# Gate scores of a recurrent attention kernel: 128 stationary columns in half of the array's rows, in place of 64x64 corners

## The chip, the core and the metric

The kernel runs on one core of a Trainium2 chip. A core has five engines with queues of their own: TensorE (PE in the profile, its weight loads PEld), VectorE (DVE), ScalarE (ACT), GpSimdE (POOL), and SyncE (SP), which issues the DMAs. The metric is the time of one execution in microseconds on the device. TensorE multiplies a stationary operand, which a load puts into its array of 128 rows and 128 columns, with a moving operand that streams through; the array can be used as a whole or in parts, of which each product names its own. Results go to PSUM, in banks of 512 fp32 numbers for each partition; VectorE and ScalarE read them there.

## What is computed

Four sequences of 768 steps, 8 heads of 40 numbers each, run through a recurrence with a matrix as its state; its output is the input of a gated MLP.

```
for t in range(S):                       # S = 768, state (B, H, D, D), D = 40
    y[:, :, t] = einsum('bhd,bhde->bhe', r_t, state)
    Sa = einsum('bhde,bhe->bhd', state, a_t)
    state = state * w_t[:, :, None, :] - einsum('bhd,bhe->bhde', Sa, b_t) \
            + einsum('bhd,bhe->bhde', v_t, k_t)
x = y, heads side by side                # (4, 768, 320)
h = gelu(x @ w_in); u, v = halves of h   # 1024 wide
out = x + (u * (w_sg @ normalised(v) + b_sg)) @ w_out
```

## The kernel before

The recurrence is cut into 12 chunks of 64 steps (`NCH`, `C`). Within a chunk the steps become matrix products: the decays w are multiplied up along the chunk, k, a and b are scaled by them, and the scores between the steps of a chunk, a 64x64 matrix for each head, give a triangular system that has to be inverted. For one chunk c and one batch b the 8 heads lie in two halves: heads 2p in partitions 0 to 63, heads 2p + 1 in partitions 64 to 127, for p = 0 to 3.

What is done for one (c, b), 48 times in all, is called a gate here, in seven pieces (`gate_1`, `gate_2`, `gate_3`, `gate_4`, `gate_a`, `gate_n`, `gate_k`; lines 248 to 301). `gate_1` to `gate_3` multiply up the decays on VectorE and write the scaled k and b side by side into one tile, `kb` (128 partitions, then pair p, then x = 0 for k and 1 for b, then 64 steps), and the scaled a into `at`. `gate_4` (line 273) is TensorE's: for each pair p and half h it multiplies k and b of that half with the scaled a of the same head, and then transposes all of `kb`. The results lie in two PSUM banks, `ab0` for the first half and `ab1` for the second: in columns 0 to 255 the scores with k (partitions 0 to 63) and with b (partitions 64 to 127), in columns 256 to 511 the transposes. `gate_a` masks the k scores on VectorE, `gate_n` writes the negated b scores into `nts` on ScalarE, where the inversion starts, and `gate_k` copies the transposes to `kbt`.

The chain from chunk to chunk (`chain1` to `chain5`, lines 417 to 497) is TensorE's too, with ScalarE and VectorE between its steps: `ru` (the right side and, with the inverse `xt`, the solution), `sp` (the new state, with `tp` its transpose), `ut`, `pq` and `yp` (the output). The inverse is built by VectorE and GpSimdE in steps on `x` with the products `tv` and `tg`, and by TensorE's `gp` and `xp`.

Every engine keeps the order in which the program is written (`InOrder`, line 112). That order comes from tables of positions: `EX`, `EW` and `T2` for the first chunks, and `GPOS` for the pieces of later gates among the chain's steps. The MLP's weights are prepared beside the last chunks, and its products (`hu`, `hv`, `sg`, `op`) follow, most of them after 400 us. A slower program for inputs out of range follows under a condition that doesn't hold here.

Every operation is recorded through one helper, so all have line 122 in the profile, and tiles tell them apart. A product of fp32 operands stands in the trace as two records, with a weight load each: `ab<-at,kb` has 1,536 records for 768 products, 32 for one gate. A transpose stands as one record, 4 for one gate. In a row's shape, `64*64 64x64` is rows and columns of the stationary operand, then partitions and columns of the moving one.

Of the kernel before, what the change touches and what calls it, by code (L numbers as in the profile page):

```python
# [18 lines left out]
C = 64  # L19
# [107 lines left out]
def engines(tc):  # L127
    nc = tc.nc
    return tuple(InOrder(tc, e) for e in (nc.vector, nc.scalar, nc.gpsimd, nc.tensor, nc.sync))
# [6 lines left out]
def attention(tc, a, xd, flag, keep, ps, mlp=None):  # L136
# [3 lines left out]
    V, A, G, T, Q = engines(tc)  # L140
    with ExitStack() as ctx:
# [101 lines left out]
        def ent(c, b):  # L243
            return (4 * c + b) % RING
# [28 lines left out]
        def gate_4(c, b):  # L273
            kb, at = gate.pop((c, b)), ats[ent(c, b)]
            ab = gate[c, b] = ps("ab0"), ps("ab1")
            for p in range(NP):
                for h in range(2):
                    r = slice(64 * h, 64 * h + 64)
                    for x in range(2):
                        T.matmul(ab[h][64 * x:64 * x + 64, C * p:C * p + C], lhsT=kb[r, p, x], rhs=at[r, p, 1],  # L280
                                 start=True, stop=True, tile_position=(64 * h, 64 * x), skip_group_check=True)
            for p in range(NP):
                T.transpose(out=ab[p // 2][:, 256 + 128 * (p % 2):384 + 128 * (p % 2)], in_=kb[:, p], identity=ident)

# [238 lines left out]
        def spread(fs, lo, hi):  # L523
            return [(lo + (hi - lo) * k / len(fs), f) for k, f in enumerate(fs)]

        PIECES = gate_1, gate_2, gate_3, gate_4, gate_a, gate_n, gate_k

        def early(c, at, X, EA, EK, w):
# [590 lines left out]
```

## Time and profile before

| | us |
|---|---|
| timed runs, median of 3 | 654.51 (654.24 to 656.18) |
| profiled execution | 661.78 |
| its span, first to last instruction | 660.0 |
| TensorE busy, products / loads | 551.5 / 493.2 |
| VectorE busy | 513.5 |
| ScalarE / GpSimdE busy | 383.3 / 372.3 |
| TensorE's mean granted clock, share of full speed | 0.905 |

The profiled execution is 7.3 us longer than the median of the timed runs; both stand here, and durations of parts come from the profiled one. Busy time counts products from the start that the profile gives to an end that it models, and products of different parts of the array overlap, so records of 218 ns can follow each other at a few ns. An idle engine's wait is put down to what ended it; "issue" says that nothing in the profile did.

### The profile page before, as it was taken

How to read it: one execution, taken by the hardware profiler on the slowest of the kernel's cores; microseconds unless marked ns; L12 is line 12 of the kernel's file. 1: busy time of each engine (PE TensorE's matmuls, PEld its weight loads, DVE VectorE, ACT ScalarE, POOL GpSimd, SP SyncE). 2: the span in 40 equal slices, each digit the busy share in tenths (PEclk: the TensorE clock that was granted, in tenths of full speed). 3: DMA queues.
4: the chain of work that ended last, by engine and by line, in shares of the span. 5: the costliest groups of instructions: out<-in, count | busy, mean ns of one | idle time of the engine just before them, and what ended most of it. 6: DMA issues, size and time to landing. Idle time of an engine off the chain costs nothing.

```text
span 660.0 us, 26858 instructions
## 1 busy us (share of the span) xinstructions
PE 551.5 (84%) x11190; PEld 493.2 (75%) x11190; DVE 513.5 (78%) x1107; ACT 383.3 (58%) x1106; POOL 372.3 (56%) x834
## 2 busy tenths in 40 slices
PE   6417878888998889888877691969999999999996
PEld 5315766776876768777767581959999999999996
DVE  7857878879888897798887659786679988767743
ACT  5627687876987778688774744564245334424410
POOL 5588587886867878678882546353322433333320
PEclk9756699989899997999978786979999999999999
DMA  7812244344344443332444331340006222000001
GB/s 234 254 58 77 78 105 109 113 121 112 99 109 112 122 117 95 97 101 76 118 110 137 83 104 55 106 129 16 31 12 199 73 89 71 32 31 0 31 25 42
DMA packets 60515, 60.77 MB, mean 92 GB/s; under 512 B 36256, under 2 KB 50336, under 8 KB 60384
## 3 DMA queue, kind: packets, MB, share of 16 engines
q1 hardware_dynamic: 60384, 58.96, 31.4%
q8 instruction: 90, 1.47, 1.0%
q14 instruction: 41, 0.34, 0.2%
HBM read 51.07 MB, written 7.86 MB: 89 GB/s over the span
## 4 chain that ended last, share of the span: by engine, by line
PE 57%; DVE 20%; ACT 10%; issue 7%; POOL 3%; DMA 1%; DVEq 0%; ACTq 0%; POOLq 0%
PE sg L122 15%; PE op L122 7%; PE hu L122 7%; PE hv L122 6%; PE ab L122 5%; PE yp L122 5%; PE pq L122 4%; PE ru L122 3%; DVE sc L122 3%; DVE x L122 2%; PE sp L122 2%; DVE at L122 2%; ACT nts L122 2%; DVE fixed L122 2%; ACT xt L122 2%
## 5 line engine op out<-in xcount | busy, mean ns | idle before, releaser
L122 POOL TENSOR_TENSOR tg<-x,n 128x56 f32<-128x56 f32 (+20 forms) x333 | 125.1, 376 | 55.4 <-ACT rhsb L122 15.3
L122 POOL TENSOR_TENSOR x<-x,tg 128x56 f32<-128x56 f32 (+20 forms) x333 | 128.2, 385 | 26.1
L122 POOL TENSOR_TENSOR gx<-g,gy 128x384 fp32r<-128x384 f32 x31 | 32.1, 1037 | 85.9 <-ACT gy L122 85.9
L122 PE MATMUL yp<-pqs,kbt 128*64 128x64 f32 x768 | 55.6, 247 | 20.2 <-DVE pqs L122 15.8
L122 PE MATMUL sg<-wsh,vh 128*128 128x384 f32 x192 | 66.3, 345 | 4.9 <-ACT vh L122 4.9
L122 PE MATMUL sg<-wsh,vl 128*128 128x384 f32 x192 | 66.2, 345 | 1.5 <-POOL vl L122 1.5
L122 ACT ACTIVATE nts<-ab 32x256 f32<-32x256 f32 x192 | 61.9, 323 | 8.1 <-DVE at L122 5.9
L122 PE MATMUL sg<-wsl,vh 128*128 128x384 f32 x192 | 65.8, 343 | 0.0
L122 PEld LDWEIGHTS yp<-pqs,kbt 128*64 128x64 f32 x768 | 45.1, 157 | 24.2 <-DVE pqs L122 16.4
L122 PE MATMUL pq<-rt,vut 128*128 128x128 f32 x384 | 59.9, 301 | 3.3 <-issue 1.8
L122 PE MATMUL ab<-at,kb 64*64 64x64 f32 x1536 | 41.7, 239 | 23.0 <-DVE kb L122 16.8
L122 ACT CAST gy<-g 128x384 fp32r<-128x384 f32 x32 | 16.4, 514 | 73.5 <-DVE g L122 73.5
L122 PEld LDWEIGHTS pq<-rt,vut 128*128 128x128 f32 x384 | 51.0, 205 | 8.1 <-issue 2.6
L122 PEld LDWEIGHTS ab<-at,kb 64*64 64x64 f32 x1536 | 34.2, 146 | 29.6 <-issue 14.6
L122 PE MATMUL yp<-rt,s 80*40 80x64 f32 x704 | 51.3, 244 | 0.0
L122 ACT CAST vh<-v 128x512 fp32r<-128x512 f32 x24 | 14.9, 620 | 57.9 <-DVE v L122 57.9
L122 ACT COPY vs<-sc 64x160 f32<-64x160 f32 x88 | 28.3, 321 | 32.6 <-DVE sc L122 31.6
L122 POOL TENSOR_TENSOR vl<-v,vh 128x512 fp32r<-128x512 f32 x24 | 31.3, 1305 | 22.7 <-ACT vh L122 22.7
L122 DVE TENSOR_TENSOR at<-ab,mask 64x256 f32<-64x256 f32 x96 | 35.7, 409 | 10.8 <-PE ab L122 10.2
L122 PEld LDWEIGHTS sg<-wsh,vh 128*128 128x128 f32 x192 | 36.8, 192 | 6.0 <-ACT vh L122 5.7
L122 DVE SCALAR_TENSOR_TENSOR g<-sg,gl,bt 128x384 f32<-128x384 f32 x32 | 19.6, 614 | 27.2 <-PE sg L122 25.3
L122 POOL TENSOR_TENSOR rs<-rs,mhalf 128x1 f32<-128x1 f32 x24 | 13.5, 561 | 48.4 <-DVE rs L122 45.6
(137 smaller groups left out, 1574.0 us busy)
## 6 DMA issues: line engine op xcount, KB each, us to landing
main<-main SPq DMA_DIRECT2D x88, 160.8 KB
vu<-vs SPq DMA_DIRECT2D x24, 160.0 KB
vs<-vb SPq DMA_DIRECT2D x24, 160.0 KB
rt<-rt SPq DMA_DIRECT2D x48, 80.0 KB
vut<-vt SPq DMA_DIRECT2D x24, 160.0 KB
xd<-yt SPq DMA_DIRECT2D x96, 40.0 KB
ws<-seq_w SPq DMA_DIRECT2D x20, 192.0 KB
xt<-xd SPq DMA_DIRECT2D x16, 192.0 KB
```

The lines of the kernel that those rows point to most:

```text
L122: return self.tc.keep_in_program_order(f(*a, **k))
```

## The change

In `gate_4` the loop over x goes. One product now takes all 128 columns of `kb` for a pair and a half, k and b together, as its stationary operand: 64 rows and 128 columns of the array, in place of a 64x64 corner for k and another for b. The result covers all 128 partitions of the bank, which puts the k scores and the b scores where they were.

```diff
             for p in range(NP):
                 for h in range(2):
                     r = slice(64 * h, 64 * h + 64)
-                    for x in range(2):
-                        T.matmul(ab[h][64 * x:64 * x + 64, C * p:C * p + C], lhsT=kb[r, p, x], rhs=at[r, p, 1],
-                                 start=True, stop=True, tile_position=(64 * h, 64 * x), skip_group_check=True)
+                    T.matmul(ab[h][:, C * p:C * p + C], lhsT=kb[r, p], rhs=at[r, p, 1],
+                             start=True, stop=True, tile_position=(64 * h, 0), skip_group_check=True)
```

On TensorE's queue, for one gate in the middle of the attention part, between the `ut` of a `chain3` and the `gp` of an inverse, there stood before (the shape is that of the result, and x2 says two equal products in a row):

```order
L122 MATMUL ut<-ident,vu_130 80x64 x4
L122 MATMUL ab_2073<-at_149,kb 64x64 x2
L122 MATMUL ab_2074<-at_149,kb 64x64 x2
L122 MATMUL ab_2073<-at_149,kb 64x64 x2
L122 MATMUL ab_2074<-at_149,kb 64x64 x2
L122 MATMUL ab_2073<-at_149,kb 64x64 x2
L122 MATMUL ab_2074<-at_149,kb 64x64 x2
L122 MATMUL ab_2073<-at_149,kb 64x64 x2
L122 MATMUL ab_2074<-at_149,kb 64x64 x2
L122 MATMUL ab_2073<-ident,kb 128x128 x2
L122 MATMUL ab_2074<-ident,kb 128x128 x2
L122 MATMUL gp<-x1z,nts_96 32x32 x32
```

and there stands now:

```order
L122 MATMUL ut<-ident,vu_130 80x64 x4
L122 MATMUL ab_1937<-at_149,kb 128x64
L122 MATMUL ab_1938<-at_149,kb 128x64
L122 MATMUL ab_1937<-at_149,kb 128x64
L122 MATMUL ab_1938<-at_149,kb 128x64
L122 MATMUL ab_1937<-at_149,kb 128x64
L122 MATMUL ab_1938<-at_149,kb 128x64
L122 MATMUL ab_1937<-at_149,kb 128x64
L122 MATMUL ab_1938<-at_149,kb 128x64
L122 MATMUL ab_1937<-ident,kb 128x128 x2
L122 MATMUL ab_1938<-ident,kb 128x128 x2
L122 MATMUL gp<-x1z,nts_96 32x32 x32
```

Nothing has changed its place, on this queue or another: each x2 of the two corners is one product of 128 result partitions, the transposes (`ident`) behind them are the same, and so are the waits. In the trace's records a gate's products go from 32 to 16, each with its load.

## Rows read from the trace of the kernel before

**Rows 1.** The page's part 1: engine, busy us (share of the span), instructions

```profile
PE 551.5 (84%) x11190; PEld 493.2 (75%) x11190; DVE 513.5 (78%) x1107; ACT 383.3 (58%) x1106; POOL 372.3 (56%) x834
```

**Rows 2.** Windows, tile ab: us, busy (count) of PE, PEld, DVE, ACT; clock, DMA

```profile
0.00:49.00 49.00, 12.07 (x288) 9.61 (x288) 5.91 (x16) 14.23 (x48) 0.73 0.60 184
49.00:77.00 28.00, 10.68 (x180) 8.37 (x180) 3.76 (x10) 8.89 (x30) 0.56 0.25 73
77.00:345.00 268.00, 49.67 (x1260) 38.06 (x1260) 26.02 (x70) 62.19 (x210) 0.95 0.40 106
```

**Rows 3.** Windows, all work, 77 to 345: PE, PEld, DVE, ACT, POOL, clock, DMA

```profile
77.00:345.00 268.00, 229.97 (x7913) 195.24 (x7914) 228.16 (x507) 208.58 (x667) 208.32 (x545) 0.95 0.40 106
```

**Rows 4.** Chain of waits, 77 to 345 us: shares of the stretch by line

```profile
by line: issue 12.1%; PE ab L122 11.2%; PE yp L122 9.1%; PE pq L122 9.0%; PE ru L122 5.5%; PE sp L122 4.6%; DVE at L122 4.0%; DVE x L122 3.5%; DVE fixed L122 3.3%; PE ut L122 3.0%; ACT xt L122 2.7%; DVE kb L122 2.6%; DVE pqs L122 2.2%; ACT 
```

**Rows 5.** Waits of PE, 77 to 345 us: us in total, times, longest

```profile
PE sp L122 <- issue: 4.7, 4, 2.0
PE ru L122 <- issue: 4.6, 10, 0.8
PE ab L122 <- issue: 3.8, 4, 1.6
PE yp L122 <- issue: 2.7, 3, 1.0
PE pq L122 <- issue: 1.8, 3, 1.3
PE gp L122 <- issue: 1.3, 2, 0.7
PE xp L122 <- issue: 0.8, 1, 0.8
```

**Rows 6.** Timeline, PE: start, length, work, records, [idle before <- releaser]

```profile
119.77 0.28 PE L122 MATMUL sp<-vu,kbt 128*32 128x40 f32 x8 [0.86 <-issue]
```

**Rows 7.** Windows, all work, between the ends of two stalls

```profile
115.67:119.77 4.10, 3.04 (x128) 2.38 (x127) 2.64 (x7) 3.61 (x12) 3.47 (x9) 1.00 0.61 178
278.49:282.58 4.09, 3.24 (x126) 2.92 (x127) 2.84 (x9) 3.40 (x10) 3.46 (x9) 1.00 0.25 64
```

**Rows 8.** DMA queues: packets, MB, share of 16 engines

```profile
q8 instruction: 90, 1.47, 1.0%
```

**Rows 9.** Timeline, PEld (weight loads) of pq and of one gate

```profile
120.33 0.97 PEld L122 LDWEIGHTS pq<-rt,vut 128*128 128x128 f32 x8
120.44 0.19 PEld L122 LDWEIGHTS pq<-rt,vut 128*128 128x128 f32 x1
121.42 0.56 PEld L122 LDWEIGHTS ab<-at,kb 64*64 64x64 f32 x32
121.47 0.21 PEld L122 LDWEIGHTS ab<-at,kb 64*64 64x64 f32 x8
122.04 0.42 PEld L122 LDWEIGHTS ab<-ident,kb 128*128 128x128 f32 x4
```

**Rows 10.** Tiles, PEld, 77 to 345 us: count, ns min/median/max, first and last start

```profile
L122 PEld LDWEIGHTS sp<-vu,kbt x1248: 106/113/172, 78.3 to 343.0; 128*32 128x32 f32 x179
L122 PEld LDWEIGHTS xp<-xt,gs x640: 102/106/111, 86.1 to 336.2; 64*32 64x32 f32 x160
L122 PEld LDWEIGHTS ab<-at,kb x1120: 129/135/136, 79.0 to 317.2; 64*64 64x64 f32 x187
L122 PEld LDWEIGHTS pq<-rt,vut x310: 186/192/338, 76.9 to 344.9; 128*128 128x128 f32 x155
```

**Rows 11.** Waits of DVE, 77 to 345 us

```profile
DVE at L122 <- PE ab L122: 6.5, 7, 1.8
```

**Rows 12.** Waits of PE and chain of waits, 0 to 77 us

```profile
PE ab L122 <- DVE kb L122: 15.5, 8, 6.7
by line: POOL x L122 12.1%; POOL tg L122 11.5%; ACT nts L122 8.4%; issue 7.3%; PE ab L122 5.8%; DVE x L122 5.1%; DMA main<-first 4.9%; DVE fixed L122 4.2%; DVE ex L122 4.2%; DVE kb L122 3.6%; ACT xt L122 3.5%; PE pq L122 3.3%; DVE n L122 2.
```

## The prediction

> **What bounds the kernel now.** I read the page first: TensorE is the busiest engine, with 551.5 of the span's 660.0 us, and VectorE is next with 513.5 [rows 1]. These are averages over very unlike stages, so I went to the stretches. The changed products are all issued in the attention part: of the 48 gates (one call of gate_4 for one chunk and one batch, 36 records each, of which 32 are the changed products and 4 are transposes) 8 lie before 49 us, 5 between 49 and 77, and 35 between 77 and 345; after 345 us there are none [rows 2]. In the stretch of 77 to 345 TensorE is busy for 230 us of 268 and VectorE for 228 [rows 3], so both are near their limit. The chain of waits for this stretch has 11.2% (30.0 us) on these tiles' products and transposes, and, larger than any engine's share, 12.1% (32 us) "issue", time in which the profile shows nothing waited for [rows 4]. The list of TensorE's waits says how much of that is TensorE's own: 27 waits in seven rows with "issue" as their releaser, 4.7 + 4.6 + 3.8 + 2.7 + 1.8 + 1.3 + 0.8 = 19.7 us, out of 268 - 230 = 38 us in which it stood idle [rows 3, 5].
>
> What these stalls are can be counted. Two that follow each other end at 115.67 and 119.77 (before the second, TensorE stood for 0.86 us), and between them TensorE took 128 products and 127 loads; between the ends at 278.49 and 282.58 it took 126 and 127 [rows 6, 7]. With the few semaphore instructions that the counts leave out, that is 256 instructions each time. The instruction queue moved 1.47 MB in 90 packets, 16 KB for each [rows 8]; over TensorE's 22,380 products and loads [rows 1] the 1.47 MB are 66 bytes for each, so a packet is about 256 of them. So I read the stalls as TensorE waiting for its next block of instructions: some 15,800 of them pass in the stretch [rows 3], 62 blocks, and 27 block ends stall, by 0.73 us on average. A busy engine is here also starved, and a change of the number of instructions counts as well as one of the work.
>
> **The change part by part.** Per gate it takes 16 products of 64 stationary columns and makes 8 of 128. In the trace each is a pair of records with a load each, so 64 instructions become 32. The moving columns (64 for each), the tiles written, the waits and the order of everything else stay. No other engine does a different thing.
>
> *Work of a gate.* Before, the four corners of the array run side by side, in eight rounds. The first loads stand at 121.42 and the next loads for the same corners at 121.47, about 0.055 later; 32 loads last 0.56 us, and without the last one's 0.14 [rows 10] the seven steps take 0.42, which is 0.060 each [rows 9]. The transposes behind them begin their loads at 122.04, so a gate's products hold TensorE for 0.62 us [rows 9]. For loads of 128 columns the nearest row is pq: its first load stands at 120.33 and its second at 120.44, 0.11 later, before the first product could stream; eight loads last 0.97, without the last one's 0.19 seven steps take 0.78, or 0.111 each [rows 9]. In pq the moving columns have doubled too, so the step alone doesn't say which of the two paces it; the first gap does, since it has only a load in it. Rows do not matter to a load: at the least and in the median, 32 columns take 106 and 113 ns with 128 rows (sp) and 102 and 106 with 64 (xp), while 64 columns take 129 and 135 and 128 take 186 and 192, some 0.9 ns for each further column [rows 10].
>
> So I take 0.11 for the first load in place of 0.055 and 0.111 for each of seven steps in place of 0.060: 0.055 + 7 x 0.051 = 0.41, say 0.42 us more per gate, 1.04 in all. The two halves of the rows still run side by side, because today's corners in both halves already do: four loads of about 0.055 fit a step of 0.060. The bounds: 0, if the 64 moving columns go on to set the step (it cannot fall below that, since there are still eight rounds of 64 columns); and, if the two halves took turns, 16 x 0.111 = 1.78 in place of 8 x 0.060 = 0.48, so 1.30 more. I take 0.42, by the nearest row.
>
> *What of it is on the path.* In 77 to 345 it is 35 x 0.42 = 14.7 us. TensorE takes its queue in order, and what it waits for there (x1z, xt, vu, s) mostly comes from engines that themselves work on its earlier products, so a later product makes those later too. The lower bound is the share that the gates' tiles have of the chain, 30.0 of their 49.7 us of TensorE time [rows 2, 4], 0.60, or 8.8 us. I take the whole. Also late are the masking of the scores on VectorE, which already waited 6.5 us for these tiles, and the negations on ScalarE behind it [rows 11]; both queues are in order, so the next chunk's kb and the products' masks behind them are late as well, which is why I allow no slack.
>
> Before 77 us, TensorE waited 15.5 us for kb, 8 times [rows 12]; that covers much. The granted clock was 0.73 before 49 us and 0.56 after [rows 2]; at half clock 0.42 becomes 0.84, so the five later gates cost up to 0.84 and the eight earlier some 0.6 each: about 9 us. The chain has 5.8% of 77 us, 4.5 us, on these tiles, out of 22.8 us of their work (12.07 + 10.68) [rows 2, 12], a fifth. I take 2 us, between 0 and 9.
>
> *Fewer instructions.* 35 x 32 = 1,120 go from the stretch, 4.4 blocks of 62. Two things follow. There are 4.4 fewer block ends, at 19.7 / 62 = 0.32 us each: 1.4 us. And time added inside a block that ends in a stall only fills the stall: 27 of 62 blocks do, so of the 35 gates about 15, each with up to 0.42: 6.4 us. Together 7.8; a stall shorter than 0.42 hides only its own length, so I take 6. The bounds are 0 and 19.7, all the stalls there are.
>
> The sum: 14.7 + 2 - 6 = +10.7 us. Its own range goes from 8.8 + 0 - 7.8 = +1 to 14.7 + 9 - 1.4 = +22. The profiled execution took 661.78 us (span 660.0), so it would take 672.5. The timed runs have a median of 654.51, 7.3 us less; the same difference put on them gives 665.2.
>
> The Trainium skill has a rule on this: "Runtime: NRT & Kernel Launch", section "Instruction fetch mechanics", has instructions come in 16 KB blocks of 256 and says that crossing a block's end is mostly hidden. The trace agrees on the size of a block and not on the cost, 27 stalls of 0.73 us. By the rule nothing would be filled, and the sum would be that of the second case below.
>
> **The rivals.** *The moving columns set the pace* (the other side). If a load of 128 columns into half of the rows hid behind two streams of 64, a gate would stay at 0.62 us and only the fetch would change: 15 gates in stalled blocks, each with 32 fewer instructions, which at the stretch's mean of 268 us for 15,800 instructions are 0.54 us of stream, capped by the stall; about 0.35 each, 5 us faster, 649.5. It decides where a load lasts under 0.06 us. Against it stands the first gap of 0.11.
>
> *The fetch gives nothing back.* Where a stall is a fixed time after the block end before, and the gates stand in blocks without one, +16.7 us: 671.2. For it: 35 of 62 block ends don't stall today. Against it: the gates are spread over all of them.
>
> *The fetch hides everything.* With relief near its bound of 19.7 the sum is about 0: 654.5. For it speaks that TensorE lost more to stalls than the gates add; against it, that a stall in one block cannot cover a gate in another.
>
> *The halves take turns.* 35 x 1.30 = 45.5 and some 5 more before 77 us: about 705. Against it are the four corners of today.
>
> **How the numbers follow.** I give the forecast 0.72, the fetch that gives nothing back 0.12, moving columns 0.08, the fetch that hides everything 0.05, and halves in turn 0.03. Differences under 0.3%, 2 us, count as none, since a measurement of this kernel can hardly tell them. Faster is the moving columns' 0.08; same is 0.05; slower is the rest, 0.87. The range goes from 656 to 677, the forecast's own low and high ends put on the timed median, and leaves out the two cases below it and the turns, 0.16, and a little of the forecast's tails.
>
> **What would show it.** The page after should have 768 records of ab with 128 columns in place of 1,536, loads of about 190 ns, the second load about 0.11 us behind the first, and some 1.04 us from a gate's first load to its transposes'. In 77 to 345 the sum of "issue" waits should fall from 19.7 to about 12, TensorE's busy share should rise, and the part after 345 should last as long as now. The forecast is wrong if the step stays at 0.06 (then faster), if it goes to 0.22 (then the halves take turns), or if the granted clock in the stretch leaves 0.95.

## The result, and the profile after

First measured: 662.27 us (median of 4 runs, 660.87 to 663.11) beside 655.10 of the kernel before (4 runs), ratio 1.0106 with an interval of 1.008 to 1.0133. In two later calls, 12 runs of the changed kernel beside 29 of the one before, the ratio was 1.0029 (0.9996 to 1.0061) and 1.0050 (1.0025 to 1.0076). In the first of these two calls (e5 to e8 below) two runs of the kernel before, one of e5 and one of e7 were over 1.5% above the fastest of their kernel; all ratios and medians here are without them. So the kernel became slower, rather by 2 to 3 us than by 7. The other runs of the kernel before lay between 653.6 and 663.0 in these calls; its execution profiled first, 661.78 us, was near the upper end. The changed kernel's first profiled execution took 663.11, only 1.3 us more.

The page's part 1 of the changed kernel (compare [rows 1]):

```profile
PE 574.2 (87%) x10422; PEld 516.7 (78%) x10422; DVE 514.8 (78%) x1107; ACT 383.1 (58%) x1106; POOL 372.3 (56%) x834
```

768 records of products fewer (384 products), 22.7 us more work of TensorE, and a span only 1.4 us longer. The rest must have been found in idle time. Where the work went, by tile ab in the windows of [rows 2] (PE, PEld, DVE, ACT; clock), and below it all work as in [rows 3]:

```profile
0.00:49.00 49.00, 19.06 (x160) 15.97 (x160) 6.17 (x16) 14.22 (x48) 0.66 0.64 184
49.00:77.00 28.00, 15.46 (x100) 13.00 (x100) 3.97 (x10) 8.47 (x29) 0.50 0.25 72
77.00:345.00 268.00, 67.91 (x700) 55.67 (x700) 26.17 (x70) 62.59 (x212) 0.95 0.40 106
77.00:345.00 268.00, 244.45 (x7419) 210.36 (x7419) 229.99 (x509) 209.81 (x674) 207.76 (x546) 0.95 0.40 106
```

After 77 us TensorE works 14.5 us more in the same 268 us, so its idle time went from 38 to 23.5. The clock there is the same 0.95; before 77 us it is lower than it was. One gate of the changed kernel on the line of weight loads (compare the gate in [rows 9]), and the loads' durations after 77 us [rows 10]:

```profile
128.79 0.97 PEld L122 LDWEIGHTS ab<-at,kb 64*128 64x128 f32 x16
129.83 0.42 PEld L122 LDWEIGHTS ab<-ident,kb 128*128 128x128 f32 x4
L122 PEld LDWEIGHTS ab<-at,kb x560: 182/188/188, 81.5 to 319.4; 64*128 64x128 f32 x187
```

From its first load to the transposes' first it takes 1.04 us; 16 loads, eight for each half of the rows, end after 0.97, so the halves do run side by side, and without the last load's 0.19 a step takes 0.111. The Trainium skill, "TensorE: Matmul & The Clock Gate", section "LDWEIGHTS (loading the stationary operand)", says that a load's time goes by its columns and not its rows; the trace agrees, 64 rows of 128 columns step as 128 rows do in pq.

The waits of TensorE named issue, 77 to 345 us, in the changed kernel (us in total, times, longest; compare [rows 5]), and its instruction queue [rows 8]:

```profile
PE ru L122 <- issue: 1.2, 3, 0.5
PE sp L122 <- issue: 1.1, 1, 1.1
PE xp L122 <- issue: 1.1, 2, 0.7
PE ab L122 <- issue: 1.0, 1, 1.0
PE yp L122 <- issue: 0.6, 1, 0.6
q8 instruction: 84, 1.38, 0.9%
```

They are 5.0 us in 8 waits, where 19.7 in 27 stood: 14.7 us less, the whole of the added work. Six blocks of 16 KB fewer are fetched. In the chain of waits the gates' tiles take the first place from issue [rows 4], and VectorE's masking waits for ab 12.8 us in 18 times, where it had 6.5 in 7 [rows 11]:

```profile
by line: PE ab L122 12.3%; PE pq L122 5.8%; issue 5.7%; DVE n L122 5.6%; ACT nts L122 4.8%; ACT gs L122 4.3%; DVE x L122 4.3%; PE ru L122 4.3%; DVE at L122 4.1%; PE yp L122 3.7%; ACT vs L122 3.6%; PE sp L122 3.5%; DVE fixed L122 3.3%; DVE x
DVE at L122 <- PE ab L122: 12.8, 18, 1.5
```

### The profile page after: what moved, and what is told of

It is laid out like the page before. It is cut to its first block, busy times and chain, and to the rows that moved or that the text cites. A ratio compares the mean times of both kernels' runs of the same rounds, so it can differ in the third digit from the quotient of the medians.

```text
span 661.4 us, 25323 instructions
## 1 busy us (share of the span) xinstructions
PE 574.2 (87%) x10422; PEld 516.7 (78%) x10422; DVE 514.8 (78%) x1107; ACT 383.1 (58%) x1106; POOL 372.3 (56%) x834
## 4 chain that ended last, share of the span: by engine, by line
PE 53%; DVE 23%; ACT 14%; issue 4%; POOL 3%; DMA 1%; DVEq 0%; SPq 0%; ACTq 0%; POOLq 0%
PE sg L122 15%; PE ab L122 7%; PE op L122 7%; PE hu L122 5%; PE hv L122 5%; PE pq L122 3%; PE yp L122 3%; ACT nts L122 3%; DVE n L122 3%; DVE x L122 3%; DVE sc L122 3%; PE ru L122 2%; ACT gs L122 2%; DVE at L122 2%; PE sp L122 2%
## 5 line engine op out<-in xcount | busy, mean ns | idle before, releaser
L122 PE MATMUL ab<-at,kb 64*128 64x64 f32 x768 | 69.5, 306 | 14.9 <-DVE kb L122 9.9
L122 PEld LDWEIGHTS ab<-at,kb 64*128 64x128 f32 x768 | 61.4, 213 | 21.2 <-ACT call L122 6.5
L122 PE MATMUL yp<-pqs,kbt 128*64 128x64 f32 x768 | 52.4, 240 | 20.5 <-DVE pqs L122 16.9
L122 PEld LDWEIGHTS yp<-pqs,kbt 128*64 128x64 f32 x768 | 41.8, 151 | 24.6 <-DVE pqs L122 17.4
L122 PE MATMUL pq<-rt,vut 128*128 128x128 f32 x384 | 58.3, 298 | 0.2
L122 ACT CAST gy<-g 128x384 fp32r<-128x384 f32 x32 | 16.4, 513 | 72.4 <-DVE g L122 72.4
L122 PE MATMUL yp<-rt,s 80*40 80x64 f32 x704 | 48.1, 236 | 0.0
L122 DVE SCALAR_TENSOR_TENSOR g<-sg,gl,bt 128x384 f32<-128x384 f32 x32 | 19.7, 615 | 26.7 <-PE sg L122 24.8
```

The lines of the kernel that those rows point to most:

```text
L122: return self.tc.keep_in_program_order(f(*a, **k))
```

## The experiments

Theory B: where TensorE takes instructions faster than they come, an instruction has a price of its own, and time added or instructions taken away give back waits one for one until none are left. Theory A: the work counts, the number of instructions little. Beside them, what the early gates cost and why. Ratios are to the kernel before in the same call, with 95% intervals; 11 or 12 runs each where nothing else is said.

| kernel | ratio | TensorE busy, 77 to 345 | issue waits there | 13th to 48th gate |
|---|---|---|---|---|
| before, first / again | 1 | 230.0 / 231.0 | 19.7 / 20.0 | 245.9 / 245.0 |
| changed, first / again / third | 1.0106 / 1.0029 / 1.0050 | 244.5 / 246.7 / 247.1 | 5.0 / 1.8 / 3.7 | 245.9 / 242.7 / 243.2 |
| e1 corners streamed twice | 1.0062 | 241.9 | 7.8 | 244.9 |
| e2 wide streamed twice | 1.0029 | 246.1 | 3.2 | 242.8 |
| e3 late gates wide | 1.0002 | 245.8 | 1.8 | 243.7 |
| e4 early gates wide | 1.0025 | 233.1 | 16.1 | 242.2 |
| e8 changed, early gates streamed twice | 1.0007 | 246.1 | 4.4 | 243.0 |
| e7 right sides in 64 | 0.9964 | 237.1 | 8.6 | 244.4 |
| e10 states in 64 | 0.9976 | 239.6 | 8.3 | 239.7 |
| e11 both in 64 | 0.9962 | 242.2 | 1.8 | 239.8 |
| e12 32 instructions more | 1.0161 | 231.7 | 25.4 | 254.9 |

All in us of one profiled execution each; issue waits are the sum of TensorE's rows of that name, the last column goes from the 13th gate's first load to the 48th's.

**The kernel before again (e6).**

> The kernel before once more, for its profile: the execution profiled first took 661.78 us, above all but the slowest of its later runs. If that one was an unlucky one, this execution is 653 to 660 us long, its first sg product starts some 3 to 5 us earlier than 430.9 us, and the waits named issue between 77 and 345 us are still well above 10 us (16 us stood in the kernel whose early gates alone have 128 columns). If instead the waits for instructions were the unlucky part, they are under 10 us here.

It took 657.39 us, its first sg product began at 426.6 (430.9 in the first). Its waits:

```profile
PE ru L122 <- issue: 5.7, 9, 1.2
PE sp L122 <- issue: 3.1, 5, 0.9
PE ab L122 <- issue: 3.1, 4, 1.1
PE xp L122 <- issue: 2.7, 2, 1.9
PE gp L122 <- issue: 2.1, 2, 1.2
PE yp L122 <- issue: 2.1, 3, 1.0
PE pq L122 <- issue: 1.2, 2, 1.0
```

20.0 us in 27, as in the first. The stalls belong to the kernel; what made the first execution long was not they.

What the waits are for stands in the traces. Counted with the semaphore instructions, the 193 waits of TensorE named issue in the 14 traces, 77 to 345 us, lie whole multiples of 256 instructions apart in each trace, to within one. And each of them ends 1.2 to 1.8 us (median 1.45) after a packet of 16 KB of the instruction queue has landed; the packet before the wait that ends at 119.77 [rows 6], for example, went from 116.93 to 118.30. In the kernel before, a packet starts 1.2 us (median) after TensorE has entered the block ahead of it and takes 1.2; with the 1.4 after the landing that is 3.8 of the 4.1 us of [rows 7]. TensorE enters 41 of its 63 blocks there no later than 1.7 us after the block's packet, as it does after all 27 waits; in the changed kernel it is 21 of 59.

**What paces a gate, and time without fewer instructions (e1, e2).** Both stream twice; e1 is shown, and e2 does the same to the changed kernel's products:

```diff
-                        T.matmul(ab[h][64 * x:64 * x + 64, C * p:C * p + C], lhsT=kb[r, p, x], rhs=at[r, p, 1],
+                        T.matmul(ab[h][64 * x:64 * x + 64, C * p:C * p + 2 * C].rearrange("p (y t) -> p y t", y=2),
+                                 lhsT=kb[r, p, x], rhs=bc(at[r, p, 1].unsqueeze(1), [64, 2, C]),
```

> The kernel before, its 64x64 corners kept, but each product streams its 64 moving columns twice (128 moving columns; the second 64 results are overwritten by the next pair's product or by the transposes, so the output stays the reference's). A gate then has as many instructions as before, and a step that should be as long as a step of 128 columns (0.111 us). Theory A (the step's length is all, instructions count little): a gate takes about 1.04 us as in the changed kernel and the time is that of the changed kernel, 662 within 2 us. Theory B (32 instructions less per gate are worth something of their own, because TensorE waits for blocks of instructions): the gate takes 1.04 us too, but the kernel is slower than the changed one by 1.4 us (fewer block ends alone) up to 8 us, so 663.5 to 670, and the waits named issue between 77 and 345 us are well above the 5 us of the changed kernel. If the second stream is free (loads pace the corners), a gate stays at 0.62 us and the time at 655.

> The changed kernel, each product streaming its 64 moving columns twice (128 moving columns, the second 64 results overwritten as in the corners' version). Theory A (the load of 128 stationary columns paces the changed gate, not the 64 moving columns): the step stays at 0.111 us, the gate at 1.04 us and the time at 662 within 2 us. Rival (the moving columns pace it or take part): the step goes to 0.16 to 0.22 us, a gate to 1.45 to 1.9 us, and the time up by 35 x 0.41 to 35 x 0.86 us, so 676 to 692.

One gate in each, on the line of loads, first e1:

```profile
125.34 0.86 PEld L122 LDWEIGHTS ab<-at,kb 64*64 64x64 f32 x32
126.38 0.31 PEld L122 LDWEIGHTS ab<-ident,kb 128*128 128x128 f32 x3 [0.17 <-issue]
```

and e2:

```profile
123.88 0.97 PEld L122 LDWEIGHTS ab<-at,kb 64*128 64x128 f32 x16
124.97 0.31 PEld L122 LDWEIGHTS ab<-ident,kb 128*128 128x128 f32 x3
```

In e2 a gate went from 1.04 to 1.09 us with twice the moving columns: the load paces it, so the first rival, with moving columns, is out. In e1 the shortest gates, with corners, take 1.03. The two differ in little but 32 instructions a gate, and e1 is the slower, 662.06 against 658.59 us, though its gates are a shade shorter. By the numbers as they were written e1 meets A (662 within 2) and misses B (663.5 and more). But these took the changed kernel for the one to compare with, and streaming twice also raised the clock in the early part (below), in both alike. Against e2, a comparison made after the fact, the 32 instructions are worth 3.5 us, inside B's 1.4 to 8. Time alone had already filled much: in e1, with as many instructions as before, issue waits fell from 20 to 7.8.

**Late or early gates alone (e3, e4).** `wide = 4 * c + b >= 13` in e3, `< 13` in e4; wide gates as in the change, the others corners.

> 128 columns only in the 35 gates that come after 77 us, corners in the first 13. Prediction's split: the late gates cost 14.7 - 6 = 8.7 us of the forecast 10.7, and the early ones 2; scaled to the 7.2 us that were measured: 5.9 late and 1.3 early, so 661. Theory E (the early gates, which cost 0.84 us each at the lower clock, make the measured loss, and the late ones are given back by fewer waits for instructions, as the two profiled executions suggest, where the lag was 3.0 us at 81.7 us and 0.9 us at 345 us): 655 to 657. Theory L (the late ones make all of it): 662.

> 128 columns only in the first 13 gates, corners in the 35 after 77 us. Prediction's split scaled to the 7.2 us: 1.3 us slower, 656.4. Theory E (the early gates make the loss): 658 to 662, and the lag of about 3 us that stands at 81 us in the changed kernel's trace stays to the end. Theory L (the late ones make all of it): 655.

e3: 657.36, 1.0002 (0.9978 to 1.0025). The 35 late gates cost nothing that shows: L's 662 and the prediction's 661 are out. It is theory E, though by its number just missed: its 655 to 657 were put on a median of 655, where the kernel before has 657.5 in this call. Its waits named issue:

```profile
PE xp L122 <- issue: 1.2, 1, 1.2
PE ru L122 <- issue: 0.3, 1, 0.3
PE yp L122 <- issue: 0.3, 1, 0.3
```

e4: 658.54, 1.0025 (0.9996 to 1.0054), 16.1 us of issue waits still there. Its 13th gate began at 72.4 us, as late as in the changed kernel (72.5, 72.4, 73.2), where before had 70.7 and 69.8. So what loss there is lies with the early gates, 1.6 us by the ratio, at E's low end, in an interval that just includes no loss. E also had the lag stay to the end, and that does not show: the 48th gate begins at 314.6 in e4, at 318.4, 315.1 and 316.4 in the changed kernel, and at 316.6 and 314.9 in the kernel before, whose own two executions differ as much. Where in the span the last 2 to 3 us are lost is open.

**The changed kernel again, and the early clock (e5, e9, e8).** e8 streams the first 13 wide gates twice.

> The changed kernel once more, in more runs and beside kernels of this call. Where the two halves of the change add up (the runs with 128 columns in the late gates alone, 1.0002 of before, and in the early gates alone, 1.0025): 1.003 of before, some 2 us slower. Where they do not add up, or the first measurement (1.0106 from 4 runs) holds: 1.008 or more, 5 us or more. The waits named issue between 77 and 345 us are 2 to 5 us in either case.

> The changed kernel a third time, in a further call. If the loss is the sum of its parts (0.0 from the late gates, 1.6 us from the early ones; 1.003 the second time), 1.001 to 1.005 of before. If the first measurement, 1.0106 from four runs of each, is right and the second one was low: 1.008 or more.

> The changed kernel with the moving columns streamed twice in the first 13 gates alone (results as before). The load paces the step, so the second stream costs no time by itself. Theory C (in the changed kernel the granted clock between 15 and 77 us is 0.50, lower than before, because TensorE streams less there; that makes the early part late by some 3 us): the clock there is 0.66 to 0.88 as in the version with all gates streamed twice, the 13th gate starts at 69.5 to 70 us in place of 72.5, and the kernel is 2 to 4 us faster than the changed kernel. Rival (the early part has slack, its clock costs nothing at the end): the time of the changed kernel within 1 us.

The repeats gave 660.15 and 660.47 us beside 659.50 and 658.14; 1.0029 and 1.0050 by ratio, or 1.9 and 3.3 us. The parts, 0 and 1.6, add up to that within the intervals. All work from 15 to 77 us (PE, PEld, DVE, ACT, POOL; clock), first of e6, the kernel before:

```profile
15.00:77.00 62.00, 32.49 (x826) 26.41 (x827) 47.50 (x106) 37.12 (x120) 43.04 (x116) 0.59 0.44 120
```

of e5, the changed one:

```profile
15.00:77.00 62.00, 38.49 (x587) 32.55 (x586) 44.41 (x99) 34.34 (x111) 41.47 (x110) 0.51 0.44 122
```

and of e8:

```profile
15.00:77.00 62.00, 32.35 (x663) 26.88 (x660) 46.17 (x104) 36.25 (x117) 42.67 (x115) 0.73 0.42 120
```

The granted clock is 0.51 in the changed kernel, which is the lower level of 1.2 GHz nearly throughout, and 0.73 with the second stream; the 13th gate comes at 70.5 in place of 72.4. The kernel took 658.66, 1.5 us less than e5 in the same call, short of C's 2 to 4 and over its rival's 1; 1.0007 (0.9978 to 1.0036) and 1.0029 overlap, so the time doesn't prove it. The traces show the lag at the 13th gate gone; at the 48th, 313.5 beside 315.1, the difference is within what one kernel's executions show. Kernels with the early gates of before have 0.54 (e3, e7) to 0.59 there, so the 0.50 to 0.51 of wide loads (e4, e5, e9) stand below them all, but not by much.

**Fewer instructions elsewhere (e7, e10, e11).** Gates stay corners. e7 changes `chain1`, e10 in the same way `chain3` (one product of `kbt[:, l0:l0 + 64]` in place of two), e11 both:

```diff
+            w = 64 if c else 32
-                for x in range(4):
-                    r = slice(32 * x, 32 * x + 32)
-                    T.matmul(ru[r, D * p:D * p + D], lhsT=at[0:k, p, x // 2, 32 * (x % 2):32 * (x % 2) + 32],
-                             rhs=vs[0:k, p, x // 2], start=True, stop=True, tile_position=(0, 32 * x), skip_group_check=True)
+                for x in range(128 // w):
+                    r, y = slice(w * x, w * x + w), w * x // 64
+                    T.matmul(ru[r, D * p:D * p + D], lhsT=at[0:k, p, y, w * x - 64 * y:w * x - 64 * y + w],
+                             rhs=vs[0:k, p, y], start=True, stop=True, tile_position=(0, w * x), skip_group_check=True)
```

> The kernel before with its gates' corners kept, but the right sides (chain1, tile ru from vs and at) of chunks 1 to 11 as products of 64 stationary columns in place of two of 32: 32 instructions less in each of 44 groups, nearly as many as the change takes from its gates. 16 loads of 64 columns last 0.55 us in yp, 32 of 32 columns some 0.28 in ru, so each group costs about 0.22 us more, 9.7 us in all, where a gate costs 0.42. Theory B (fewer instructions give back what TensorE waits for blocks, up to 16 us): 9.7 - 16 = 6 us faster than before, 651.5 beside 657.5, waits named issue under 5 us. Theory A (instructions count little): 5 to 10 us slower, 663 to 667.

> The kernel before with its gates' corners kept, and the products of the state (chain3, tile sp) as 64 stationary columns in place of two of 32: 32 instructions less in each of 44 groups. 32 loads of 32 columns last 0.37 us there, 16 of 64 columns 0.55 in the right sides, so +0.18 us a group, 8 us in all. Theory B (blocks of instructions): the waits named issue fall from 20 to about 9 us as they did with the right sides in 64 columns, and the kernel is 0.995 to 0.999 of before. Theory A (instructions count little): 1.010 to 1.012.

> Right sides and states both in 64 columns, gates in corners as before: 64 instructions less per chunk and batch, 9.7 + 8 = 17.7 us more of TensorE's work. If what fewer instructions give back is bounded by the stalls there are (20 us, of which 8.6 were left with the right sides alone), the second half buys at most 8.6 - 2 = 6.6 us for 8: the kernel is 0.5 to 3 us slower than with the right sides alone, 0.998 to 1.001 of before, waits named issue 2 to 4 us. If each block of instructions saved is worth the same without a bound, it is twice as good as the right sides alone: 0.993.

e7: 657.03 beside 659.50, 0.9964 (0.9927 to 1.0002), with 6 us more work of TensorE. A's 5 us slower is out; B has the sign, at 2.5 us by the medians in place of 6, in an interval that just includes no gain. Its issue waits:

```profile
PE sp L122 <- issue: 2.6, 4, 1.0
PE yp L122 <- issue: 2.3, 3, 1.2
PE ab L122 <- issue: 1.9, 1, 1.9
PE ru L122 <- issue: 1.6, 4, 0.6
PE gp L122 <- issue: 0.2, 1, 0.2
```

8.6 us, where B had under 5; they fell by 11.4, more than the 6 us of work could fill. e10: 0.9976 (0.9953 to 1.0000), 8.3 us, as B had it. e11: 656.38 beside 658.14, 0.9962 (0.9932 to 0.9992), faster than before and than the changed kernel; two waits are left:

```profile
PE yp L122 <- issue: 1.1, 1, 1.1
PE sp L122 <- issue: 0.7, 1, 0.7
```

Twice the saving did not give twice the gain (656.38 beside e10's 656.27): what can be given back is bounded by the stalls. The bound's own number, 0.998 to 1.001, was missed on the fast side; the 0.993 of no bound lies at the interval's very edge. In e10 and e11 the 48th gate comes some 5 us sooner after the 13th, and the kernel ends only 2 us sooner; what takes the rest back after 311 us was not followed up.

**More instructions (e12, 6 runs).** In the late gates of the kernel before, ahead of the transposes:

```diff
+            for i in range(8 if 4 * c + b >= 13 else 0):
+                h, y = i % 2, i // 2
+                r = slice(64 * h, 64 * h + 64)
+                T.matmul(ab[h][32 * y:32 * y + 32, 256:264], lhsT=kb[r, 0, 0, 0:32], rhs=at[r, 0, 1, 0:8],
+                         start=True, stop=True, tile_position=(64 * h, 32 * y), skip_group_check=True)
```

> The kernel before, its corners kept, with 8 products of 32 stationary and 8 moving columns more in each of the 35 gates after 77 us, into columns that the transposes overwrite: 32 instructions more per gate, as many as the change takes away there. Their own time, from xp (64 loads of that form begin within 0.54 us): 16 of them 0.135 us, 4.7 us in all. Theory B (between two waits for instructions 256 pass in 4.1 us, 16 ns each, and a gate's 32 are worth 0.51 us wherever TensorE is behind): 35 x 0.51 = 17.9 us where every block is behind, 7.8 where only the 27 of 62 blocks that stall today are, so 8 to 18 us slower than before, and the waits named issue up from 20 to 24 to 33 us. Theory A (only the work counts): 0 to 4.7 us slower, the waits named issue at or under 20 us.

669.39 us beside 659.17 (11 runs), 1.0161 (1.0120 to 1.0203). B's 8 to 18 us holds, A's 4.7 does not:

```profile
PE ru L122 <- issue: 9.2, 11, 1.8
PE sp L122 <- issue: 7.1, 5, 3.3
PE yp L122 <- issue: 3.6, 4, 1.4
PE ab L122 <- issue: 2.3, 5, 0.7
PE xp L122 <- issue: 1.5, 2, 0.8
PE pq L122 <- issue: 1.1, 2, 0.7
PE gp L122 <- issue: 0.6, 2, 0.4
```

The sum is 25.4 us in a window that holds fewer gates than before, since the gates come later. But the products' own time was put too low. One gate (compare [rows 9]):

```profile
128.64 0.81 PEld L122 LDWEIGHTS ab<-at,kb 64*64 64x64 f32 x48
129.47 0.42 PEld L122 LDWEIGHTS ab<-ident,kb 128*128 128x128 f32 x4
```

The shortest gates hold TensorE for 0.83 us in place of 0.63, 7.0 us in 35 gates; were it all on the path, A would come close below the interval, which begins at 7.9 us. What speaks against A is e1. From the 13th gate to the 48th, TensorE's busy time rose by 12.0 us in e1, the issue waits fell by 11 to 12 (to 7.1 from 19.2 and 18.0), and the stretch, 244.9, was no longer than before; in e12 busy time rose by 8.7, the waits by 2.5 to 3.7 (to 21.7), and the stretch by 9 to 10. In this stretch time alone is taken up by the waits, and time that comes with instructions is not. (The 4 us that e1 loses all the same lie elsewhere and were not located.) Over 1,120 instructions the 10.2 us are 9 ns each, their own work included.

## Why the prediction was right in sign, and where it was off

*What bounds the kernel.* Right: TensorE is bound by its work and by the arrival of its instructions together. e12 added instructions, and the waits rose in spite of the work that came with them; e7 took instructions away from another place, and they fell by more than its added work. That the waits are for blocks of 256 rested on the counts of [rows 7]; the packets' times in all the traces (under e6) bear it out.

*Work of a gate.* Right. 0.42 was forecast; the shortest gates went from 0.625 to 1.038 us, 0.413. The 35 later gates added 14.5 to 17 us of TensorE's busy time, against 14.7.

*The early gates.* Not contradicted at 2 us: e4 has 1.6, in an interval that just includes no loss. What the forecast didn't have is that their clock would fall too, from 0.59 to 0.51; with the wide loads the gates there went from about 1.06 to 1.9 us (medians).

*Fewer instructions.* This step failed. The term was -6, its bound -19.7, and about 12 us of waits were to be left, where 5.0 were; the waits fell by 14.7 in the first pair and by 16 to 18 in the repeats. Two assumptions made it small. First, that only the blocks whose end shows a wait have a stall to fill, 15 of the 35 gates at 0.42. In the trace of before 15 gates do lie in such blocks, but 24 lie in blocks after which TensorE went on no later than 1.7 us behind the next packet, as it does after a wait. That these too were held by the fetch is the likeliest reading, and 24 x 0.42 are 10 us; e1 shows that time added in every gate, without one instruction less, took 12 us out of the waits. Second, a saved instruction was priced over all blocks, 1.4 us for 4.4 of them. Where TensorE is behind, [rows 7] had the price: 256 in 4.1 us, 16 ns each, 0.51 us for a gate's 32, which with 0.42 of work is 0.93 us a gate and 33 us for 35, more than all stalls there were; at the 9 ns of e12 it is still 25. So the bound was the better guess, and the rival in which the fetch hides everything, given 0.05, is what the late gates did: e3, 1.0002.

*The sum.* With sizes from the middle of those measured: 15.5 + 2 - 16 = +1.5 us, beside 1.9 and 3.3 us in the repeats and 7.2 in the first four runs. The profiled pair differs by 1.3 us where the forecast had 10.7, and nearly all of that is the error of the one term. The time 665.2 came out only 2.9 us above the 662.27 first measured by luck, because another error ran against it: the execution of before that was profiled was a long one, and its 7.3 us over the median were taken off, while the changed kernel's profiled execution (663.11, not 672.5) lies 0.8 us above its own median. Why the first four runs gave 7 us, and why runs of one kernel differ by up to 10, was not found.

*The rule of the Trainium skill* ("Runtime: NRT & Kernel Launch", section "Instruction fetch mechanics", crossing a block's end is mostly hidden) does not hold in this stretch: by it e12 would have cost at most its own 7.0 us, in place of 10.2, and e7 would have been slower.

*The rivals with moving columns and with halves in turn* fell by the gate's 1.04 us and by e2.

## What to carry to other kernels

Where a queue of small products waits with nothing named as releaser, count the instructions between two such waits; if it is one number and its multiples, look for the packets of the instruction queue, price an instruction at no more than that pace (16 ns here; e12's came to 9 with their own work), and count added work there as free until the waits are used up. Take instructions out where a wider load costs least: 32 instructions cost 0.42 us of TensorE in the gates, and by an estimate from the loads' rows about 0.2 in the right sides and the states; the late gates alone came out at 1.0002, the right sides and states together at 0.9962 (0.9932 to 0.9992). Measure a change of half a per cent in more runs than four.

## What was not expected of the hardware

The same products, streamed twice, ran sooner: between 15 and 77 us the granted clock was 0.51 with 64 moving columns per load of 128 and 0.73 with 128, and TensorE's busy time fell from 38.5 to 32.4 us. And TensorE lost 20 us in 268 to waits that all end 1.2 to 1.8 us after a packet of its instructions landed, while that queue's packets took only 1.0% of the DMA engines' time [rows 8].
